# One byte copied in place of a shift and a masked merge in the narrowing of 64-bit weights, with a new order of all operations

## The chip, the cores and the metric

One core of a Trainium2 chip runs the whole program in one launch. The metric is the device time of an execution in microseconds, and less is better. The kernel is written for the engines directly: TensorE (PE) multiplies, VectorE (DVE), ScalarE (ACT) and GpSimd (POOL) do the elementwise work, and SyncE (SP) issues the DMAs.

## The reference, cut to what matters

Three layers run one after the other on 2 x 768 tokens:

```
attn:  q, k, v (2, 8, 768, 64): a window of +-15 keys, and 24 key sums (max over 32 keys) and value
       sums (mean) as extra columns; softmax; times v
moe:   x @ w_gate (4 experts, best 2 kept); q, k, v = x @ wq, wk, wv; causal softmax attention for
       every expert; times wo; the two kept experts are added with their softmaxed gates
moe2:  xk, xr = mixes of x and the previous token; k = max(xk @ w_k, 0); v = k*k @ w_v
       r = sigmoid(xr @ w_r); out = r * v
```

The three weights of the last layer, `w_k` (512 x 1024), `w_v` (1024 x 512) and `w_r` (512 x 512), reach the kernel as 64-bit floats, two 32-bit words each. The other inputs are 32-bit floats.

## The kernel before

The program builds a list of 2056 operations, each with the engines that could do it (its "ways"), and then issues them in an order written out by hand in `ORDER`. An entry is 4 times the number of the operation plus the number of the way: 770 is operation 192 in its third way, which is POOL. Each engine runs its own operations in that order and waits only where an operation needs another engine's result. `HOMES` gives the buffer slot of each tile. So `ORDER` sets which engine does what, and who queues behind whom; the costs written beside the operations were used to make it and are not read at run time.

The work has three stages. First the windowed attention (`stage1_*`, lines 570 to 700), tile by tile of 128 tokens. For a tile, PE makes the scores (line 583, or lines 588 and 589 for the first three tiles), DVE adds the mask and takes the maximum (line 606), ACT takes the exponentials (line 609), DVE sums and inverts (lines 612 and 614), any of three engines normalizes (lines 620 and 625), PE transposes (line 637), DVE and ACT copy the result out of PSUM (lines 368 and 369), and PE multiplies by the values (line 679). The value sums are copied into the value tiles (lines 534, 535 and 537) before that last product. Then the projections (lines 754 and 772) and the experts' attention (lines 854, 952, 994), interleaved with the rest of the first stage. Last the third layer: `w_r` (line 1146), `w_k` (line 1197) and `w_v` (line 1284), the last two as products of halves that save one multiplication in eight.

Every product of the second and third stage is made of three matmuls of rounded parts: a value x is split into a rounded high part and the low rest, by `halves` (a rounding copy, then a subtraction). PE is used in four shapes: whole (the projections and the last stage), by rows (lines 637 and 854), by halves (lines 679 and 952) and by quarters (lines 500, 583, 588, 589). A wait of PE at a step of the start is met by the operations of that step: the first projection, operation 256 (line 772), needs the high and low part of tile 0 (operations 124 and 125) and of its weight (29 and 30); operations 257 and 258 need 31 to 34. Operation 194, the value product of tile 2, needs the copies 192 and 193 of the value sums.

`raw64` (line 1014) makes 32-bit floats out of 64-bit ones. There are 20 pieces of 128 x 512 weights, four of `w_r`, eight of `w_k` and eight of `w_v`. For each piece it loads pairs of words, takes the magnitude of the high word, scaled (ACT, line 1035), bounds it (DVE or POOL, lines 1037 and 1038), shifts the low word right by 29 so that its last three bits are left (DVE, line 1041), merges the sign of the high word in (DVE, line 1043), and shifts the magnitude left by 3 and merges the two (DVE, line 1045). The split into parts follows.

Of the kernel before, what the change touches and what calls it, by code (L numbers as in the profile page):

```python
# [45 lines left out]
SIGN = -0x80000000  # L46
# [9 lines left out]
    12, 0, 4, 16, 36, 44, 24, 32, 56, 52, 64, 20, 60, 236, 72, 40, 92, 48, 244, 201, 68, 28, 188, 280, 100, 792,  # L56
    240, 650, 284, 272, 1238, 296, 108, 276, 206, 380, 304, 256, 300, 248, 288, 96, 308, 264, 1242, 292, 104, 646,
    210, 252, 260, 328, 268, 512, 440, 80, 408, 444, 400, 432, 404, 312, 464, 316, 412, 392, 332, 324, 424, 436,
    416, 76, 652, 384, 396, 548, 564, 428, 320, 572, 112, 336, 516, 388, 340, 532, 524, 420, 472, 88, 704, 790, 556,
    552, 468, 448, 540, 528, 452, 84, 344, 696, 348, 568, 456, 476, 576, 148, 352, 712, 356, 544, 680, 460, 560,  # L60
    360, 796, 216, 368, 480, 373, 365, 664, 520, 960, 484, 604, 536, 600, 622, 688, 489, 168, 1244, 580, 584, 848,
    590, 592, 613, 492, 976, 672, 656, 618, 1288, 609, 824, 1264, 748, 220, 117, 744, 132, 140, 496, 624, 121, 228,
    125, 1272, 136, 500, 773, 232, 129, 757, 1024, 770, 629, 760, 1028, 753, 764, 1032, 840, 144, 808, 1268, 856,
    776, 844, 632, 154, 812, 816, 676, 1036, 157, 780, 1048, 860, 1052, 162, 784, 820, 1056, 1060, 1296, 828, 164,
    1280, 1072, 668, 1068, 832, 1076, 708, 1304, 964, 1080, 716, 1164, 174, 1040, 952, 684, 1256, 1084, 968, 800,
    660, 1188, 1092, 1276, 224, 180, 1192, 804, 177, 196, 852, 1212, 980, 184, 192, 836, 1140, 212, 1088, 700, 1248,
    1144, 932, 864, 1044, 1252, 868, 1148, 877, 880, 692, 1152, 1260, 740, 872, 720, 724, 1064, 1168, 1300, 1157,
    1284, 1216, 728, 956, 3596, 1308, 1332, 1292, 1336, 596, 1160, 1506, 1357, 1172, 1312, 1316, 1220, 736, 1341,
    972, 732, 1326, 984, 1176, 1349, 504, 1196, 1362, 1353, 1180, 1224, 1344, 1501, 1525, 1320, 1200, 1229, 884,
    1520, 888, 1184, 1204, 892, 946, 1232, 1364, 904, 1208, 901, 948, 908, 897, 1852, 1369, 913, 1476, 1096, 1376,  # L70
    918, 1856, 1480, 1380, 1832, 1860, 1485, 938, 1489, 1528, 1497, 1864, 1372, 940, 1492, 1964, 1836, 1868, 1812,
    1572, 1840, 3600, 920, 1540, 992, 1968, 1844, 1816, 3605, 1556, 1824, 1548, 1508, 1820, 924, 1564, 1972, 1588,
    1828, 1580, 1384, 1552, 1532, 928, 1512, 1544, 2004, 1388, 1516, 1568, 988, 1584, 3608, 1576, 1104, 2192, 1000,
    1420, 1592, 1444, 2196, 3612, 1848, 2168, 1536, 1412, 3628, 1404, 1392, 1428, 2216, 2008, 1468, 1448, 2172,
    1560, 1436, 636, 1100, 1408, 2012, 2176, 640, 1109, 1432, 1396, 2180, 1472, 1872, 1596, 1400, 3616, 1612, 1924,
    2016, 1928, 1117, 1904, 1900, 1941, 3622, 1424, 2185, 996, 1416, 1004, 1917, 8, 1112, 1908, 3692, 1600, 1120,
    1936, 2188, 2200, 1912, 1328, 1009, 1440, 3640, 2204, 508, 1124, 3644, 2220, 2208, 1452, 1604, 2224, 1021, 1932,
    1876, 1944, 1128, 1456, 1976, 2212, 1984, 1017, 1608, 3632, 1672, 1988, 1013, 2020, 1992, 1787, 1464, 2760,
    1996, 1724, 1700, 1692, 1980, 1647, 1132, 1921, 1764, 2000, 1137, 1760, 1732, 1460, 1684, 2228, 1696, 1708,
    1791, 2024, 2768, 1769, 2240, 1776, 1880, 1756, 1712, 2764, 2244, 3624, 1780, 2248, 2028, 2776, 2233, 2252,  # L80
    1716, 1736, 1676, 1886, 2236, 1651, 2772, 1620, 2056, 2257, 1624, 1773, 2052, 3636, 1616, 1680, 2380, 3704,
    1629, 3648, 1640, 2068, 1948, 2033, 1633, 2400, 3654, 2432, 2072, 2065, 1636, 2416, 1688, 2038, 2384, 1728,
    1888, 3656, 1704, 1652, 1893, 1720, 2424, 2408, 2388, 1740, 2392, 1792, 1896, 1744, 1668, 2440, 1656, 1752,
    1952, 2060, 2260, 2444, 2080, 1808, 2076, 1796, 1660, 1748, 2780, 1664, 2396, 1800, 2464, 2092, 2512, 2096,
    1958, 1804, 2788, 2084, 2088, 2404, 3660, 2784, 2792, 3696, 4444, 2540, 2472, 2800, 2468, 2428, 4540, 2820,
    2524, 3701, 2548, 2481, 2796, 2477, 2100, 2484, 2812, 2556, 2488, 2572, 2564, 2436, 2828, 2576, 2516, 2816,
    2492, 3708, 2532, 2116, 2412, 2804, 3712, 2832, 2420, 2808, 2824, 1960, 2040, 2264, 2836, 2268, 2048, 2840,
    2560, 3718, 2272, 2536, 2844, 2312, 2448, 2497, 2044, 3720, 2276, 2848, 2852, 2316, 2452, 2104, 2320, 2500,
    2856, 2288, 2292, 2281, 2324, 2544, 2296, 2552, 2329, 2916, 2284, 2568, 3672, 2912, 2892, 2460, 2888, 2933,
    3028, 2929, 2904, 2332, 2921, 2520, 2925, 2456, 2968, 2908, 2964, 3032, 2896, 2900, 2300, 2981, 3036, 4448,  # L90
# [1397 lines left out]
```

## Time and profile before

| | |
|---|---|
| time, median of 3 runs | 333.66 us (333.64 to 333.79) |
| the profiled execution | 332.78 us, of which 331.0 us from its first to its last instruction |
| PE busy | 319.1 us, 96% |
| DVE busy | 311.3 us, 94% |
| ACT busy | 266.8 us, 81% |
| POOL busy | 114.0 us, 34% |
| HBM | 30.16 MB read, 3.15 MB written |
| granted TensorE clock, 331.0 us | 1.000 |

The shares are averages over the stages. A busy PE may still have gaps between matmuls, since the ends of matmuls are modelled; whether it has any is seen from the time that a run of equal matmuls takes.

### The profile page before, as it was taken

The numbers are of one execution on the slowest core, as the hardware profiler recorded it, in microseconds if no ns is written. First come the engines' busy times: TensorE is split into PE (matmuls) and PEld (weight loads), VectorE is DVE, ScalarE is ACT, GpSimd is POOL, SyncE is SP. The second block draws the span as 40 slices with busy tenths as digits, with TensorE's granted clock in tenths as the row PEclk, the third lists the DMA queues.
The fourth block names the chain that finished last, engine by engine and source line by source line (L and its number), as shares of the span: only waits on it lengthen the run. The fifth ranks groups of instructions, "written<-read, shape, count | busy, mean of one in ns | idle before, by whom it ended". The sixth has DMA issues, their size and how long they took to land.

```text
span 331.0 us, 8978 instructions
## 1 busy us (share of the span) xinstructions
PE 319.1 (96%) x3296; PEld 286.8 (87%) x3296; DVE 311.3 (94%) x941; ACT 266.8 (81%) x777; POOL 114.0 (34%) x127
## 2 busy tenths in 40 slices
PE   3979999999999999999999999999999999999995
PEld 2869988888789879787776899999998899999995
DVE  3789999999999899989999999999999999999996
ACT  0989999999898779779887889889799988965360
POOL 0556872768303810432310001545036000360231
PEclk9999999999999999999999999999999999999999
DMA  7996985757242000111212001100050000021033
GB/s 247 400 395 204 305 301 189 270 152 248 92 137 64 4 0 10 59 63 65 87 43 63 3 4 61 63 0 3 0 183 10 0 0 2 18 79 52 0 113 128
DMA packets 19628, 34.08 MB, mean 103 GB/s; under 512 B 2080, under 2 KB 8480, under 8 KB 19584
## 3 DMA queue, kind: packets, MB, share of 16 engines
q1 hardware_dynamic: 19584, 33.51, 30.0%
q8 instruction: 26, 0.43, 0.5%
q14 instruction: 18, 0.15, 0.1%
HBM read 30.16 MB, written 3.15 MB: 101 GB/s over the span
## 4 chain that ended last, share of the span: by engine, by line
PE 94%; DVE 2%; DMA 2%; SPq 1%; issue 0%; ACT 0%; ACTq 0%
PE ps L1284 18%; PE ps L1197 18%; PE ps L754 11%; PE ps L1146 10%; PE ps L637 6%; PE ps L952 6%; PE ps L772 6%; PE ps L854 6%; PE ps L994 5%; PE ps L679 3%; PE ps L583 3%; DMA ks<-in_kS 2%; PE ps L588 1%; PE ps L500 1%; DVE w L606 1%; SPq L359 1%
## 5 line engine op out<-in xcount | busy, mean ns | idle before, releaser
L1284 PE MATMUL ps<-w,s 128*128 128x256 f32 x336 | 48.7, 281 | 0.0
L1284 PEld LDWEIGHTS ps<-w,s 128*128 128x128 f32 x336 | 43.9, 188 | 0.1
L1197 PE MATMUL ps<-b,w 128*128 128x384 f32 x216 | 40.3, 337 | 0.0
L1197 PEld LDWEIGHTS ps<-b,w 128*128 128x128 f32 x216 | 38.0, 188 | 0.1
L368 ACT ACTIVATE t<-ps 128x192 f32<-128x192 f32 (+1 forms) x108 | 30.9, 356 | 8.6 <-PE ps L637 4.2
L754 PE MATMUL ps<-b,w 128*128 128x384 f32 x192 | 36.6, 341 | 0.0
L1146 PE MATMUL ps<-w,b 128*128 128x512 f32 x144 | 35.8, 398 | 0.0
L754 PEld LDWEIGHTS ps<-b,w 128*128 128x128 f32 x192 | 33.2, 188 | 0.9 <-issue 0.4
L1146 PEld LDWEIGHTS ps<-w,b 128*128 128x128 f32 x144 | 26.5, 188 | 5.9 <-DVE gsum L820 0.2
L609 ACT ACTIVATE w<-w,nm 128x120 f32<-128x120 f32 x72 | 28.5, 407 | 0.9 <-DVE nm L606 0.7
L368 ACT ACTIVATE b<-ps 128x384 f32<-128x384 f32 (+4 forms) x50 | 23.8, 492 | 3.9 <-PE ps L994 1.6
L368 ACT ACTIVATE s<-u 128x512 fp32r<-128x512 f32 x24 | 14.8, 628 | 9.4 <-DVE u L1059 5.5
L1123 DVE SCALAR_TENSOR_TENSOR t<-b,mu,t 128x384 f32<-128x384 f32 x32 | 21.2, 681 | 0.8 <-ACT t L387 0.7
L854 PE MATMUL ps<-ks,b 64*128 64x384 f32 (+3 forms) x192 | 21.8, 342 | 0.0
L368 ACT ACTIVATE w<-ps 120x256 f32<-120x256 f32 (+2 forms) x49 | 19.7, 445 | 1.7 <-PE ps L1146 0.8
L952 PE MATMUL ps<-t,b 128*64 128x384 f32 (+2 forms) x144 | 20.7, 422 | 0.0
L376 DVE TENSOR_TENSOR b<-t,b 128x384 fp32r<-128x384 f32 x37 | 20.1, 567 | 0.5 <-ACT b L368 0.3
L772 PE MATMUL ps<-q,b 128*128 128x260 f32 x144 | 20.3, 290 | 0.2 <-DVE b L376 0.2
L772 PEld LDWEIGHTS ps<-q,b 128*128 128x128 f32 x144 | 18.2, 188 | 1.6 <-issue 0.5
L368 ACT ACTIVATE b<-t 128x384 fp32r<-128x384 f32 x38 | 19.0, 516 | 0.5 <-PE ps L1197 0.5
L994 PE MATMUL ps<-u,w 128*128 128x384 f32 x96 | 18.9, 338 | 0.0
L387 ACT ACTIVATE t<-b,omu 128x384 f32<-128x384 f32 x28 | 16.9, 613 | 2.2 <-PE ps L952 1.6
(202 smaller groups left out, 913.4 us busy)
## 6 DMA issues: line engine op xcount, KB each, us to landing
s<-in_wk SPq DMA_DIRECT2D x8, 512.0 KB, 4.0
s<-in_wv SPq DMA_DIRECT2D x8, 512.0 KB, 4.2
w<-in_vp SPq DMA_DIRECT2D x15, 256.0 KB, 6.5
w<-in_qT SPq DMA_DIRECT2D x12, 256.0 KB, 5.6
out_y<-t SPq DMA_DIRECT2D x24, 128.0 KB, 1.8
s<-in_wr SPq DMA_DIRECT2D x4, 512.0 KB, 5.7
s<-in_kS SPq DMA_DIRECT2D x6, 320.0 KB, 4.7
ks<-in_kS SPq DMA_DIRECT2D x4, 400.0 KB, 3.9
```

The costliest lines, as they stand in the source:

```text
L368: ways = [("act", act(n, sb), lambda: nc.scalar.activation(dst(), src(), AF.Copy)), ("dve", dve2(n) if sb else dve(n), lambda: nc.vector.t ...
L376: ways = [("dve", dve(n), lambda: nc.vector.tensor_tensor(dst(), a(), b().bitcast(F32), ALU.subtract), sb)]
L609: op("act", act(NK, True) + 186, lambda i=i, z=z, pr=pr, nm=nm: nc.scalar.activation(pr()[:, i], pr()[:, i], AF.Exp, bias=nm.t[:, i:i + 1] ...
L754: mm(p.t[:, :C], a[kc].t[:, cols], x.t[:, kc, :], start=(kc == 0 and i == 0), stop=(kc == KC - 1 and i == 2))
L772: mm(p.t[:, :260], x.t[:, kc, tok], a[kc].t, start=(kc == 0 and i == 0), stop=(kc == KC - 1 and i == 2))
L854: mm(ps[e2].t[:, :z - a], q1.t[r, x, tok], ks.t[r, y, a:z], start=n == 0, stop=n == 2)
L952: mm(acc.t[64 * e2:64 * e2 + 64, tq0 * P:(tq0 + cnt) * P], vv.t[:, kb, e * D:(e + 1) * D], th[e2].t[:, i0 * P:(i0 + cnt) * P], start=first ...
L994: mm(p.t[:, :C], a[ep].t[:, m * P:(m + 1) * P], x.t[:, ep, :], start=(ep == 0 and i == 0), stop=(ep == 1 and i == 2))
L1123: op("dve", dve(C) + 60, lambda: nc.vector.scalar_tensor_tensor(tmp(), cur(), mu.t[:, i:i + 1], tmp(), ALU.mult, ALU.add), r=rd, w=[(mb, m ...
L1146: mm(p.t, a.t[:, kc, tok], w[2](), start=(kc == 0 and i == 0), stop=(kc == KC - 1 and i == 2))
L1197: mm(p.t[:, :C], a[2]()[:, o:o + P], x.t[:, u, j], start=not (j or i), stop=j == 1 and i == 2)
L1284: mm(p.t[:, :256], x.t[:, u, j * P:(j + 1) * P], v[2]()[:, col:col + 256], start=not (j or i), stop=j == FC // 2 - 1 and i == 2)
```

## The change

Two edits, one in `raw64` and one in `ORDER` and `HOMES`.

In `raw64` a new operation copies the top byte of the low word over the lowest byte of the high word, after the magnitude has been taken from it. The three wanted bits then stand in the high word beside the sign, and one instruction with two steps (shift right by 5, and a mask for the sign and the last three bits) replaces the shift and the merge. So a piece still has five operations: magnitude, bound, byte copy, shift and mask, last merge. The byte copy may go to ACT, POOL or DVE.

```diff
-        def low():
-            return raw.t[:, :, 0]
-
...
-        op("act", act(512, True) + 60, lambda: nc.scalar.activation(ff(), high(), AF.Abs, scale=F64_SCALE),
+        op("act", 660, lambda: nc.scalar.activation(ff(), high(), AF.Abs, scale=F64_SCALE),
            r=[raw], w=[(fg, 0)])
...
-        op("dve", dve2(512), lambda: nc.vector.tensor_scalar(g(), low(), 29, None, ALU.logical_shift_right),
-           r=[raw], w=[(fg, 1)], lock=True)
-        op("dve", dve(512), lambda: nc.vector.scalar_tensor_tensor(
-            g(), raw.t[:, :, 1], SIGN, g(), ALU.bitwise_and, ALU.bitwise_or), r=[raw], w=[(fg, 1)], lock=True)
+        def half(i):
+            return raw.t.bitcast(mybir.dt.uint8)[:, :, i]
+
+        any_of("act", [("act", 680, lambda: nc.scalar.activation(half(4), half(3), AF.Copy)),
+                       ("pool", pool_ts(512), lambda: nc.gpsimd.tensor_copy(half(4), half(3))),
+                       ("dve", dve2(512), lambda: nc.vector.tensor_copy(half(4), half(3)), True)], w=[raw])
+        op("dve", dve2(512), lambda: nc.vector.tensor_scalar(g(), raw.t[:, :, 1], 5, SIGN + 7, ALU.arith_shift_right,
+                                                             ALU.bitwise_and), r=[raw], w=[(fg, 1)], lock=True)
```

`ORDER` and `HOMES` are new throughout. The list of operations is the same but for the two above. Of its 20 byte copies the new order gives 11 to ACT, 7 to POOL and 2 to DVE. 231 of the 2056 operations change their engine, in all directions, and the counts of operations go from 781 to 778 on DVE, 579 to 567 on ACT and 123 to 138 on POOL. PE has the same 458 operations; it changes between its four shapes 81 times instead of 87, and from operation 194 on (the same 26 operations of PE lie before it in both orders) 71 times instead of 78.

The start of the new order, up to operation 194 (entry 776), against the old (entry 776 too):

```diff
-    12, 0, 4, 16, 36, 44, 24, 32, 56, 52, 64, 20, 60, 236, 72, 40, 92, 48, 244, 201, 68, 28, 188, 280, 100, 792,
-    240, 650, 284, 272, 1238, 296, 108, 276, 206, 380, 304, 256, 300, 248, 288, 96, 308, 264, 1242, 292, 104, 646,
-    210, 252, 260, 328, 268, 512, 440, 80, 408, 444, 400, 432, 404, 312, 464, 316, 412, 392, 332, 324, 424, 436,
-    416, 76, 652, 384, 396, 548, 564, 428, 320, 572, 112, 336, 516, 388, 340, 532, 524, 420, 472, 88, 704, 790, 556,
-    552, 468, 448, 540, 528, 452, 84, 344, 696, 348, 568, 456, 476, 576, 148, 352, 712, 356, 544, 680, 460, 560,
-    360, 796, 216, 368, 480, 373, 365, 664, 520, 960, 484, 604, 536, 600, 622, 688, 489, 168, 1244, 580, 584, 848,
-    590, 592, 613, 492, 976, 672, 656, 618, 1288, 609, 824, 1264, 748, 220, 117, 744, 132, 140, 496, 624, 121, 228,
-    125, 1272, 136, 500, 773, 232, 129, 757, 1024, 770, 629, 760, 1028, 753, 764, 1032, 840, 144, 808, 1268, 856,
-    776, 844, 632, 154, 812, 816, 676, 1036, 157, 780, 1048, 860, 1052, 162, 784, 820, 1056, 1060, 1296, 828, 164,
...
+    12, 0, 16, 36, 44, 24, 32, 56, 52, 64, 20, 188, 236, 96, 40, 68, 48, 244, 205, 72, 28, 104, 209, 280, 60, 1238,
+    240, 284, 304, 650, 272, 92, 788, 202, 380, 276, 288, 248, 292, 256, 100, 264, 4, 260, 646, 296, 1242, 252, 108,
+    268, 308, 328, 512, 300, 432, 424, 436, 464, 408, 312, 400, 428, 316, 384, 412, 76, 652, 324, 440, 392, 444,
+    416, 556, 220, 388, 532, 794, 516, 420, 80, 472, 524, 320, 704, 396, 332, 548, 336, 564, 404, 112, 340, 572,
+    344, 520, 656, 448, 552, 452, 88, 348, 680, 352, 460, 540, 536, 664, 560, 712, 84, 356, 576, 468, 373, 456, 688,
+    528, 796, 148, 360, 368, 544, 672, 568, 365, 952, 476, 1244, 489, 486, 580, 960, 480, 584, 8, 696, 600, 840,
+    604, 590, 593, 168, 492, 1356, 216, 618, 1296, 613, 496, 622, 848, 609, 744, 808, 500, 748, 133, 196, 118, 624,
+    764, 137, 125, 224, 121, 773, 129, 1024, 142, 629, 757, 1028, 760, 753, 1032, 768, 660, 632, 144, 676, 776, 668,
...
```

In it the first slab copies on ACT are operations 51 and 52 instead of 50; the normalization 148 of tile 2 (entry 593) is on DVE instead of POOL, the copy 192 (entry 768) too; the roundings 33 and 35 of the first weights leave DVE for ACT and POOL, and the subtraction 34 comes to DVE from POOL.

## Rows read from the trace of the kernel before

**Rows 1.** The page, busy time of PE and DVE: us, share, instructions.
```profile
PE 319.1 (96%) x3296; PEld 286.8 (87%) x3296; DVE 311.3 (94%) x941; ACT 266.8 (81%) x777; POOL 114.0 (34%) x127
```
**Rows 2.** Windows: PE, PEld, DVE, ACT, POOL busy (instructions), clock, DMA share, GB/s.
```profile
30.00:45.00 15.00, 15.00 (x162) 14.15 (x160) 14.50 (x47) 14.19 (x61) 10.89 (x12) 1.00 0.85 286
...
210.00:225.00 15.00, 15.00 (x87) 15.00 (x86) 15.00 (x31) 12.35 (x28) 6.22 (x5) 1.00 0.00 1
```
**Rows 3.** The chain that ended last, from the first weights on: start us, us, what.
```profile
196.28 54.67 PE ps L1197 x312
...
266.91 2.85 PE ps L1284 x24
...
270.45 56.77 PE ps L1284 x480
327.25 0.43 DVE t L1170
327.70 0.43 DVE t L1059
```
**Rows 4.** Groups by shape: x count, busy us, mean ns, idle before.
```profile
L1043 DVE SCALAR_TENSOR_TENSOR s<-s,s 128x512 int32<-128x512 int32 x20 | 14.7, 736 | 0.0
L1035 ACT ACTIVATE s<-s 128x512 f32<-128x512 f32 x20 | 13.5, 684 | 1.3 <-POOL q L378 1.3
L1041 DVE TENSOR_SCALAR s<-s 128x512 int32<-128x512 int32 x20 | 8.5, 436 | 0.0
L371 POOL TENSOR_SCALAR w<-s 128x512 fp32r<-128x512 f32 x12 | 8.2, 685 | 4.2 <-DVE rse L885 2.3 <-DVE s L1045 1.7
L1038 POOL TENSOR_SCALAR s<-s 128x512 f32<-128x512 f32 x2 | 3.8, 1922 | 2.5 <-PE ps L637 1.4 <-ACT s L1035 1.1
L620 DVE TENSOR_TENSOR w<-w,rss 128x480 f32<-128x480 f32 x1 | 0.7, 657 | 0.0
```
**Rows 5.** Line 1045: ns least/median/most, first and last start in us.
```profile
L1045 DVE SCALAR_TENSOR_TENSOR s<-s x20: 675/688/1475, 54.6 to 260.5; 128x512 int32<-128x512 int32 x20
```
**Rows 6.** The chain, runs of equal matmuls with and without a change of shape.
```profile
37.83 0.61 PE ps L637 x16
...
44.22 0.47 PE ps L637 x16
...
100.24 2.10 PE ps L754 x12
...
106.88 2.30 PE ps L754 x12
```
**Rows 7.** Timeline of ACT, 9 to 11 us: start us, us, engine, line.
```profile
10.06 0.74 ACT L368 ACTIVATE s<-ks 128x640 f32<-128x640 f32 x1
```
**Rows 8.** The chain, 20 to 30 us.
```profile
20.50 0.72 DVE w L534
...
24.33 0.42 DVE q L369 x2
24.74 0.91 DVE q L376
...
25.86 0.61 DVE b L376
26.51 1.53 PE ps L772 x9
28.05 1.08 PE ps L679 x32
```
**Rows 9.** Timeline of DVE, 23 to 28 us, with the idle time before an instruction.
```profile
23.63 0.28 DVE L606 CUSTOM_DVE_ANT_0 w<-ps,msk 128x120 f32<-128x120 f32 x1 [0.74 <-PE ps L583]
...
24.66 1.00 DVE L376 TENSOR_TENSOR q<-b,q 128x260 fp32r<-128x260 f32 x1
...
26.39 0.73 DVE L376 TENSOR_TENSOR q<-b,q 128x260 fp32r<-128x260 f32 x1
```
**Rows 10.** Timeline of POOL, 24 to 27 us.
```profile
24.62 0.75 POOL L378 TENSOR_TENSOR q<-b,q 128x260 fp32r<-128x260 f32 x1 [1.16 <-DVE q L369]
```

260 rows, old and new, of tables (HOMES, ORDER) are left out of this document.

## Prediction

> **What bounds the kernel now.** Three views, in this order. The page's busy shares give PE 96% and DVE 94% [rows 1], which leaves open which of the two sets the end. The windows narrow it: between 30 and 45 us, and again between 210 and 225 us, PE is busy for all of 15.00 us, and DVE for 14.50 and 15.00 us [rows 2]. A busy PE can still hide gaps, so the third view decides, the chain that ended last. In it 312 matmuls of 384 columns take 54.67 us, 0.175 us each, and 480 of 256 columns take 56.77 us, 0.118 us each [rows 3]. The same 0.175 us holds far ahead of that stage: 12 matmuls of line 754 take 2.10 us at 100.24 us [rows 6], when DVE's queue holds quite other work. A rate that is the same in stages with different company is PE's own rate, not a wait on DVE. So from about 29 us to 327.25 us PE runs back to back, and what is left outside are the start (PE reaches its first projection at 26.51 us and waits between its runs before that) [rows 8] and the end: two DVE instructions of 0.43 us [rows 3] and the last DMA, up to 331.0 us.
>
> From this follows the rule for all that comes: an edit is worth what it changes in the length of PE's own queue, in the start, or in the end. A saving on DVE is worth nothing unless PE waited for it.
>
> **The change in raw64.** It takes away 20 merges of line 1043, 0.736 us each, 14.7 us of DVE [rows 4]. The shift of line 1041 (0.436 us) becomes a shift with a mask on the same tile; I leave its price at 0.436 us, since the words read and written are as many. It adds 20 byte copies of 128 x 512. None is in the trace, so bounds: the nearest row for ACT is line 1035, which reads the same pairs of words (0.684 us); for POOL line 371 with 0.685 us below and line 1038 with 1.922 us above; for DVE 0.436 us of line 1041 below and 0.736 us of line 1043 above [rows 4]. I take 0.68 us on ACT, 0.69 on POOL (a copy is nearer to line 371 than to the bounding of line 1038) and 0.44 on DVE. That gives 11 x 0.68 = 7.5 us more on ACT, 7 x 0.69 = 4.8 us on POOL, 2 x 0.44 = 0.9 us on DVE. The new order then moves other work: 781 operations of DVE become only 778, so most of the 14.7 us is filled again.
>
> On the path to the end this is worth 0. What hides it is PE itself, saturated. The new copy also lengthens the chain of one piece, since it must wait for the magnitude, and the shift for the copy: at most 0.68 + 0.44 = 1.1 us [rows 4], less what the bound beside them takes. The cover: the last piece's line 1045 starts at 260.5 us [rows 5], and its stage begins on PE at 266.91 us [rows 3], which leaves 6.4 us for the merge and the splits behind it. If that cover were gone, it would cost 1.1 us once.
>
> **PE's queue in the new order.** PE has the same 458 operations, so only the changes of shape differ. Their price: 16 transposes of line 637 take 0.61 us with a whole-array run behind them and 0.47 us with a run by rows behind them, and 12 matmuls of line 754 take 2.30 us after transposes and 2.10 us among their like [rows 6]. So a change costs between 0.14 and 0.20 us. From operation 194 on the new order has 71 changes where the old has 78. 7 x 0.14 = 0.98 us less; with 0.20 it would be 1.4 us, and nothing if the new places make PE wait. I take 0.98 us, the nearer price for a change by itself, because only about half of the changes enter a whole-array run.
>
> **The start.** In both orders the same 26 PE operations come before operation 194 (line 679, at 28.05 us now), so it is a fair mark. DVE sets it. Up to the subtraction 125 (25.86 us now) both queues hold, from the first reduction of line 612 on, 25 maxima, 3 reductions with their reciprocals, 4 copies of value sums, 2 copies of transposes and one copy of line 534. The old one holds besides two weight roundings (0.42 us) and a subtraction (0.91 us) [rows 8]; the new one a normalization (0.66 us) [rows 4]. That is 0.42 + 0.91 - 0.66 = 0.67 us earlier. Against it, ACT makes two slab copies ahead of the exponentials of tile 0 and not one; a copy holds ACT for 0.64 us (10.06 to 10.70; the row's 0.74 us overlaps the next) [rows 7], so the first reduction starts 0.64 us later. The two cancel. The idle 0.74 us of DVE at 23.63 us [rows 9] may go or stay, since the scores that ended it stand earlier in PE's queue now.
>
> Behind 125 the new DVE queue is longer: 125 itself, the subtractions 34, 30 and 32, the rounding 157, and the copy 192, for which PE's operation 194 waits. With 0.61 us for a large one [rows 8], 0.65 us for a subtraction of weights undisturbed (0.73 us in the row, less the overlap) [rows 9] and 0.72 us for line 534 [rows 8]: 0.61 + 3 x 0.65 + 0.61 + 0.72 = 3.89 us. From 25.86 us this ends at 29.75 us, 1.70 us after the 28.05 us at which PE starts operation 194 now; without DVE's idle time (0.74 us, and 0.28 us spread ahead of it) it would end at 28.73 us, 0.68 us later. I take 0.6 us as the loss, near that lower end, because the wait at 23.63 us came from scores that PE now has done by then. Both ends stay: a gain of some 0.4 us, if DVE is as early and the three subtractions interleave better, to a loss of 1.7 us. What is late next is DVE's operation 158, for operation 262 of PE; the 1.08 us of operation 194 [rows 8] hide its 0.61 us.
>
> **The end.** The new order also closes with a sum and a product on DVE after the last PE operation. The last but one operation of PE leaves DVE the same two, 2 x 0.43 us [rows 3], which fit into the last one's 12 x 0.118 = 1.4 us. So 0 us, and no more than 0.9 us late if DVE came with two instructions of arrears.
>
> **Sum.** Against the profiled execution's 332.78 us (331.0 us of span and 1.8 us around it): 0 - 0.98 + 0.6 + 0 = -0.4 us, 332.4 us. The median of the runs shown is 333.66 us, 0.9 us above that execution, so the forecast for it is 333.3 us. That is 0.1% faster, and what a measurement of this kernel can tell from no change is about 0.2%, 0.67 us: forecast no change.
>
> **Rivals.**
> The start costs nothing: the copy 192 comes in time and only the changes of shape count, 333.66 - 0.98 - 0.3 = 332.4 us. For it: DVE loses its 0.74 us wait. Against: 3.89 us of DVE's work stand between the start of 125 and operation 194, where now operation 194 starts 2.2 us behind it (25.86 to 28.05 us) [rows 8].
>
> DVE was the bound after all: then part of 14.7 us comes back. In the rows DVE is idle for nothing at 210 to 225 us [rows 2], so it can't be excluded by its own share; the equal 0.175 us speaks against it. With one in seven of the 14.7 us on the path, 333.3 - 2.1 = 331.2 us; I give it less than a tenth.
>
> Slower, by POOL's byte copy: if it is like line 1038, 1.92 us, a copy is 1.23 us above my price. Five of the seven stand early, beside PE's runs between about 45 and 105 us, when POOL also makes the normalizations that PE waits for soonest. Between 30 and 45 us POOL is idle for 4.1 us [rows 2], so one or two are absorbed; where two stand directly ahead of a normalization PE waits 2 x 1.23 = 2.5 us: 333.3 + 2.5 = 335.8 us. It decides once such a copy is longer than about 1.4 us, twice line 371. Against it: a copy has no arithmetic, and the two calls of line 1038 in the old order did no harm.
>
> Slower, by DVE and POOL at once: of two equal subtractions of line 376 one took 1.00 us [rows 9] while POOL's line 378 ran beside it [rows 10], the other 0.73 us [rows 9], and line 1045 has a median of 688 ns and a most of 1475 ns [rows 5]. With 0.27 us more for each of the three subtractions of the start and 0.27 us for the copy 192, the loss there is 0.6 + 1.08 = 1.7 us: 333.66 - 0.98 + 1.7 = 334.4 us. POOL has 15 operations more. The Trainium skill has a rule for it (GPSIMD Engine Reference, "8. Key points"): GpSimd shares its SBUF interfaces with VectorE, and they contend when VectorE reads two inputs from SBUF or runs in a mode with both ports. By that rule, the change removes 20 two-input instructions and adds 7 GpSimd ones; the rows agree that such a slowdown exists.
>
> That the bits are not as meant (the mask cut to the sign alone) would change the result's last bits and no time.
>
> **How the numbers follow.** Forecast case, 333.3 us, its own range 332.6 to 334.0 us: 0.50, of which 0.10 faster, 0.38 the same, 0.02 slower. Start free: 0.20, 0.19 of it faster and 0.01 the same. DVE bound: 0.08, faster. POOL copy: 0.10, slower. DVE beside POOL: 0.12, of which 0.09 slower and 0.03 the same. So faster 0.37, same 0.42, slower 0.21. The range leaves out DVE as the bound (0.08) and the POOL copy's upper part (0.10): 332.0 to 334.9 us.
>
> **What would show it.** PE again at 0.175 and 0.118 us a matmul in the long runs, and no line 1043 of a merge: DVE busy down by only a few us, ACT's about the same. The run of line 679 before the long projections at 28.7 us, held by DVE's line 534. POOL's byte copies at 0.7 us, ACT's at 0.68 us. From there on less than 1 us gained to the last matmul, which then ends near 326.9 us, and 3.8 us from it to the end. The prediction is wrong if PE's idle time appears between 30 and 185 us, if the byte copies on POOL pass 1.4 us, or if the long runs of PE themselves get shorter per matmul.

## The result, and the profile after

The new kernel takes 335.48 us (median of 6 runs, 335.16 to 336.59) where the kernel before takes 333.65 us beside it (332.56 to 334.64). The ratio is 1.0064, 95% interval 1.0039 to 1.0089: it is 0.6% slower. The forecast was 333.3 us and no change, with a range that ended at 334.9 us.

The profiled execution has a span of 333.6 us, 2.6 us more than before. First the busy times of its page, in the form of [rows 1]:

```profile
PE 318.0 (95%) x3296; PEld 287.4 (86%) x3296; DVE 310.1 (93%) x938; ACT 274.7 (82%) x763; POOL 119.7 (36%) x142
```

DVE was relieved of 14.7 us of merges and yet has only 1.2 us less to do. The windows, with the columns of [rows 2], show two of its stretches again and two later ones:

```profile
30.00:45.00 15.00, 15.00 (x168) 14.31 (x164) 14.41 (x53) 14.46 (x64) 8.58 (x10) 1.00 0.71 229
210.00:225.00 15.00, 15.00 (x87) 15.00 (x86) 15.00 (x32) 12.85 (x28) 5.55 (x4) 1.00 0.00 0
220.00:240.00 20.00, 20.00 (x116) 20.00 (x115) 20.00 (x42) 19.14 (x40) 6.54 (x6) 1.00 0.08 27
240.00:260.00 20.00, 19.24 (x98) 17.14 (x97) 19.93 (x39) 18.03 (x35) 3.78 (x4) 1.00 0.16 54
```

The last stretch in the kernel before:

```profile
240.00:260.00 20.00, 20.00 (x103) 18.30 (x102) 20.00 (x43) 19.33 (x42) 8.23 (x4) 1.00 0.25 80
```

Where nothing waits, PE keeps its pace (87 matmuls in 15 us, as in [rows 2]). Between 240 and 260 us it is idle for 0.76 us, where it was never idle before, while DVE is busy for 19.93 of the 20. So DVE and PE are both full there, and a late DVE shows. The groups by shape, as in [rows 4]:

```profile
L1040 ACT ACTIVATE s<-s 128x512 uint8<-128x512 uint8 x11 | 15.2, 1379 | 0.2
L1045 DVE SCALAR_TENSOR_TENSOR s<-s 128x512 int32<-128x512 int32 x20 | 14.1, 708 | 0.1
L1031 ACT ACTIVATE s<-s 128x512 f32<-128x512 f32 x20 | 13.6, 684 | 0.7 <-DVE s L1043 0.7
L1041 POOL COPY s<-s 128x512 uint8<-128x512 uint8 x7 | 9.8, 1393 | 5.4 <-ACT s L1031 2.7 <-issue 2.5
L1043 DVE TENSOR_SCALAR s<-s 128x512 int32<-128x512 int32 x20 | 9.4, 469 | 1.5 <-ACT s L1040 0.7 <-POOL b L987 0.4 <-POOL s L1041 0.3
...
L1042 DVE COPY s<-s 128x512 uint8<-128x512 uint8 x2 | 1.5, 748 | 0.0
```

A byte copy costs 1.38 us on ACT, 1.39 on POOL and 0.75 on DVE, about twice what I had put in on each engine. On DVE it costs what the removed merge cost (0.736 us). The chain that ended last, in the form of [rows 3], is no longer PE's at the end but DVE's, back to where the view could follow it:

```profile
322.14 1.43 DVE t L1059
323.57 0.60 DVE s L375
...
329.52 0.42 DVE t L1059
329.94 0.34 DVE t L1170
330.29 0.02 issue
330.31 0.42 DVE t L1059
```

The timeline of PE in three places (start, length, and in brackets the idle time before it with what ended it):

```profile
27.81 1.45 PE L771 MATMUL ps<-q,b 128*128 128x260 f32 x9
29.50 1.15 PE L678 MATMUL ps<-w,u 120*64 120x64 f32 x32 [0.24 <-DVE u L533]
...
95.57 0.80 PE L753 MATMUL ps<-b,w 128*128 128x384 f32 x3 [0.47 <-DVE nm L860]
...
325.71 2.99 PE L1284 MATMUL ps<-w,s 128*128 128x256 f32 x24
```

With these rows the 2.6 us of this pair of executions split into three. Operation 194 starts at 29.50 us where it was 28.05 us [rows 8]: +1.45. From there to PE's end (327.22 us before, 328.70 us after) it takes 299.20 us (328.70 less 29.50) where it took 299.17 (270.45 + 56.77 less 28.05) [rows 3, 8]: +0.03. From PE's end to the end of DVE's last instruction it takes 2.03 us (330.73 less 328.70) where it took 0.91 [rows 3]: +1.12.

The +0.03 in the middle is no sign that nothing happened there. The windows from operation 194 to PE's end, first before, then after:

```profile
28.05:327.22 299.17, 299.16 (x2831) 270.25 (x2831) 291.40 (x840) 249.15 (x709) 101.59 (x103) 1.00 0.25 80
29.50:328.70 299.20, 297.98 (x2831) 270.50 (x2831) 289.00 (x837) 256.51 (x694) 107.88 (x117) 1.00 0.24 78
```

PE's busy time became 1.18 us shorter (299.16 to 297.98 us), and PE now stands idle for 1.22 us, where it stood idle for 0.01 us. The 1.22 us are three waits: 0.47 us at 95.57 us, 0.52 us at 243.02 us (ended by ACT, whose copy before had itself waited 0.31 us for DVE's line 1045) and 0.24 us at 252.61 us. The timelines of POOL and DVE in the new kernel say what happens to DVE:

```profile
92.56 1.37 POOL L1041 COPY s<-s 128x512 uint8<-128x512 uint8 x1
93.74 1.02 POOL L377 TENSOR_TENSOR u<-t,u 128x384 fp32r<-128x384 f32 x1
...
239.14 1.64 POOL L377 TENSOR_TENSOR w<-s,w 128x512 fp32r<-128x512 f32 x1 [1.75 <-ACT w L367]
...
321.99 1.29 POOL L377 TENSOR_TENSOR s<-b,s 128x512 fp32r<-128x512 f32 x1 [4.93 <-ACT s L367]
```

```profile
93.96 1.07 DVE L1043 TENSOR_SCALAR s<-s 128x512 int32<-128x512 int32 x1 [0.27 <-POOL s L1041]
...
239.08 0.54 DVE L375 TENSOR_TENSOR b<-t,b 128x384 fp32r<-128x384 f32 x1
239.55 1.65 DVE L1123 SCALAR_TENSOR_TENSOR t<-b,mu,t 128x384 f32<-128x384 f32 x1
...
322.06 1.51 DVE L1059 TENSOR_TENSOR t<-t,w 128x256 f32<-128x256 f32 x1
```

Lay the two side by side. At 322.06 us a DVE product that takes 0.42 us elsewhere starts 0.07 us behind a POOL subtraction and takes 1.51 us: it ends 0.29 us after POOL does. At 239.55 us another ends 0.42 us after POOL's. Such an instruction makes little headway until POOL is done. In the whole trace of the new kernel 44 DVE instructions with two SBUF inputs start with more than 0.2 us of a POOL instruction still to run, and 19 of them are more than 0.15 us longer than the median of their shape; of the 75 that read PSUM and start so, none is. The Trainium skill states this as an exclusive lock (SBUF — State Buffer, "Who interferes with whom"): of the pair of ports that VectorE and GpSimd share, the engine that issues first keeps it for its whole instruction and the other is blocked when VectorE runs in a mode with both ports, and VectorE with two SBUF inputs contends with a GpSimd instruction that reads SBUF. The trace agrees, at 1.51 us against 0.42; the subtraction there is the only POOL instruction between 318 and 327 us. Where POOL's instruction comes second, it is POOL that waits: its product at 264.66 us takes 5.21 us, where one of the same shape at 249.27 us takes 0.73 us, and DVE's subtractions beside it keep their 0.68 us. Most of the 25 that were not held stand beside such a waiting POOL instruction.

```profile
264.66 5.21 POOL L1060 TENSOR_TENSOR s<-s,s 128x256 f32<-128x256 f32 x1 [14.66 <-DVE s L1059]
```

By 95.57 us it has reached PE: the shift with mask waits for POOL's byte copy (0.27 us), is held by POOL's next subtraction (1.07 us for 0.42), the maximum of line 860 behind it is late, and PE waits 0.47 us.

### The profile page after: what moved, and what is told of

It reads as the page before. It is cut to its first block, busy times and chain, and to the rows that moved or that the text cites. A ratio compares the mean times of both kernels' runs of the same rounds, so it can differ in the third digit from the quotient of the medians.

```text
span 333.6 us, 8972 instructions
## 1 busy us (share of the span) xinstructions
PE 318.0 (95%) x3296; PEld 287.4 (86%) x3296; DVE 310.1 (93%) x938; ACT 274.7 (82%) x763; POOL 119.7 (36%) x142
## 5 line engine op out<-in xcount | busy, mean ns | idle before, releaser
L1197 PE MATMUL ps<-b,w 128*128 128x384 f32 x216 | 41.0, 338 | 0.5 <-ACT b L367 0.5
L753 PE MATMUL ps<-b,w 128*128 128x384 f32 x192 | 37.1, 341 | 0.5 <-DVE nm L860 0.5
L367 ACT ACTIVATE t<-ps 128x192 f32<-128x192 f32 (+1 forms) x94 | 27.3, 343 | 4.7 <-PE ps L636 3.5
L608 ACT ACTIVATE w<-w,nm 128x120 f32<-128x120 f32 x72 | 27.7, 394 | 0.0
L377 POOL TENSOR_TENSOR b<-t,b 128x384 fp32r<-128x384 f32 x7 | 8.4, 1201 | 38.3 <-ACT b L367 38.3
L1060 POOL TENSOR_TENSOR t<-t,w 128x256 f32<-128x256 f32 x7 | 9.8, 1398 | 31.2 <-DVE t L1059 11.1
L375 DVE TENSOR_TENSOR b<-t,b 128x384 fp32r<-128x384 f32 x37 | 20.9, 574 | 0.0
L367 ACT ACTIVATE w<-ps 120x256 f32<-120x256 f32 (+2 forms) x47 | 18.6, 438 | 1.9 <-PE ps L1146 0.9
L377 POOL TENSOR_TENSOR w<-s,w 128x512 fp32r<-128x512 f32 x12 | 16.4, 1364 | 10.2 <-ACT w L367 7.3
L993 PE MATMUL ps<-u,w 128*128 128x384 f32 x96 | 19.7, 341 | 0.0
L853 PE MATMUL ps<-ks,b 64*128 64x384 f32 (+3 forms) x192 | 19.5, 335 | 0.0
```

The lines of the kernel that those rows point to most:

```text
L367: ways = [("act", act(n, sb), lambda: nc.scalar.activation(dst(), src(), AF.Copy)), ("dve", dve2(n) if sb else dve(n), lambda: nc.vector.t ...
L375: ways = [("dve", dve(n), lambda: nc.vector.tensor_tensor(dst(), a(), b().bitcast(F32), ALU.subtract), sb)]
L377: ways.append(("pool", pool_tt(n), lambda: nc.gpsimd.tensor_tensor(dst(), a(), b().bitcast(F32), ALU.subtract)))
L608: op("act", act(NK, True) + 186, lambda i=i, z=z, pr=pr, nm=nm: nc.scalar.activation(pr()[:, i], pr()[:, i], AF.Exp, bias=nm.t[:, i:i + 1] ...
L753: mm(p.t[:, :C], a[kc].t[:, cols], x.t[:, kc, :], start=(kc == 0 and i == 0), stop=(kc == KC - 1 and i == 2))
L993: mm(p.t[:, :C], a[ep].t[:, m * P:(m + 1) * P], x.t[:, ep, :], start=(ep == 0 and i == 0), stop=(ep == 1 and i == 2))
```

## The experiments

Theories. A: the byte copy's double price. B: the new order's start. C: DVE is a bound beside PE, so what is added to it shows. D: C, and POOL takes from DVE beside it as much as it takes off it. E: the new order's count of DVE work alone. Every ratio is to the kernel before, timed on the same chip. The kernel before had medians of 333.65 to 334.05 us beside these runs, so two kernels that were not timed side by side are better compared by their ratios than by their medians; where the two differ, both are given. The new kernel has 1.0064 (1.0039 to 1.0089).

**The copy at the price assumed (e1_word_copy).**

```diff
-            return raw.t.bitcast(mybir.dt.uint8)[:, :, i]
+            return raw.t[:, :, 1].bitcast(F32)
```

> The new kernel with its order, but each of the 20 copies takes the high word onto itself (4 bytes an element, 128x512) and not one byte; left out: the three last bits of the low word, so the last bits of the weights are not the reference's. The instruction count, the engines and the waits stay. Theory A (the byte copy's price: 1.38 us on ACT, 1.39 on POOL, 0.75 on DVE in the new kernel, twice what I had put in): the word copy takes 0.7 us on ACT and POOL and 0.4 on DVE, the waits of PE at 94, 242 and 252 us and the late DVE at the end go, and the time falls by 1.0 to 2.6 us from the new kernel's 335.5 us, to 332.9 to 334.5 us. Theory B (the order itself: its start, 1.5 us later at operation 194, and DVE's arrears at the end): the copies get cheaper but the time stays within 0.5 us of 335.5 us.

Measured: 335.10 us, 1.0027 (1.0003 to 1.0052). The groups and PE at 95 us:

```profile
L1042 ACT ACTIVATE s<-s 128x512 f32<-128x512 f32 x11 | 7.5, 686 | 0.2
L1043 POOL COPY s<-s 128x512 f32<-128x512 f32 x7 | 4.9, 704 | 5.2 <-ACT s L1033 2.7 <-issue 2.5
```

```profile
95.13 0.80 PE L755 MATMUL ps<-b,w 128*128 128x384 f32 x3
```

The wait at 95 us is gone, those at 242 and 252 us and the late end stay. The intervals of the two ratios overlap, so the 0.4% between them is a likely part of the loss and not proved by this run.

**The edit alone (e2_old_order_new_edit).** Old `ORDER` and `HOMES`, the copy issued right behind its magnitude:

```diff
-    ... 900 (magnitude) ... 902 (shift) ... 903 (merge) ...
+    ... 900 (magnitude), 902 (byte copy) ... 903 (shift with mask) ...
```

> The old order and homes with the new raw64: the byte copies stand right behind their magnitude, on the same engines as in the new order (11 ACT, 7 POOL, 2 DVE), and the shift with mask stands where the merge stood. DVE loses 20 x 0.736 us of merges and gains 2 x 0.75 us. Theory A (byte copy's price): ACT gains 15 us and POOL 10 us in an order that has no room made for them, and the time rises to 334.5 to 337 us. Theory B (the order): the edit by itself costs and brings nothing, 333.2 to 334.0 us, as the kernel before (333.65 us). Theory C (DVE is a bound after all): its 13 us less show as a gain, below 333.0 us.

Measured: 347.72 us, 1.0416 (1.0381 to 1.0450). All three theories missed the size. By its page DVE is busy for 303.2 of 345.2 us, idle for 42.0, where it was idle for 19.7 before [rows 1]. The place that shows how, POOL, DVE and PE at 61 to 65 us:

```profile
61.32 1.31 POOL L1043 COPY s<-s 128x512 uint8<-128x512 uint8 x1 [1.63 <-issue]
```

```profile
62.66 1.06 DVE L1045 TENSOR_SCALAR s<-s 128x512 int32<-128x512 int32 x1 [2.55 <-DMA w<-in_qT]
```

```profile
64.12 0.96 PE L855 MATMUL ps<-ks,b 64*128 64x512 f32 x5 [2.14 <-DVE nm L862]
```

The bracket names a DMA, but the instruction starts as POOL's copy ends (62.63 us): that copy it waited for. Before, shift and merge needed only the load and ran whenever DVE's queue came to them; now DVE stands still in its queue until another engine has copied, and PE behind it. The edit is not free by itself: in the old order, with the copy put right behind its magnitude, it costs 14 us.

**The order alone (e3_new_order_old_edit).** Shift and merge of the old `raw64` in the new order.

```diff
-        any_of("act", [... half(4), half(3) ...], w=[raw])
-        op("dve", ... 5, SIGN + 7, ALU.arith_shift_right, ALU.bitwise_and) ...
+        op("dve", ... raw.t[:, :, 0], 29, None, ALU.logical_shift_right) ...
+        op("dve", ... g(), raw.t[:, :, 1], SIGN, g(), ALU.bitwise_and, ALU.bitwise_or) ...
```

> The new order and homes with the old raw64: shift and merge on DVE, no byte copies. Against the new kernel ACT loses 15 us and POOL 10 us of copies and DVE gains 20 x 0.736 - 2 x 0.75 = 13.2 us. Theory A (byte copy's price on ACT and POOL): the waits for ACT at 242 and 252 us go, 333.0 to 334.5 us, as DVE's share of 93% leaves room. Theory B (the order's start): no change from the new kernel, 335.2 to 335.8 us. Theory C (in the new order DVE has no room, as its 2.2 us behind the last matmul say): PE waits for DVE in the stretch of the weights and the time rises by 3 to 13 us, to 338.5 to 348 us.

Measured: 345.03 us, 1.0331 (1.0299 to 1.0363), theory C's range. From 200 to 250 us its windows give

```profile
200.00:250.00 50.00, 46.98 (x266) 46.02 (x264) 49.72 (x93) 40.74 (x86) 16.14 (x12) 1.00 0.07 22
```

3 us of PE idle beside a full DVE. Of 13.2 us more on DVE, 9.6 us came out as time by the medians (345.03 less 335.48), 8.9 us by the ratios. In this kernel DVE has little room left.

**Bounds left out (e5_no_bound_new, e6_no_bound_old).** The other direction: DVE's load made less.

```diff
-        any_of("dve", [("dve", dve2(512), lambda: nc.vector.tensor_scalar(ff(), ff(), F64_TOP, None, ALU.min), True),
+        any_of("dve", [("dve", dve2(512), lambda: None, True),
```

> The new kernel without the 18 bounds of the magnitude that its DVE makes (line 1033, 0.488 us each, 8.8 us; 5 of them, 2.1 us, behind 199 us, where DVE is never idle). Left out: the bound, which only acts on weights out of range. Theory C (DVE paces the last third of the new kernel: it ends 2.2 us behind the last matmul, and PE waits for it at 242 and 252 us): the time falls by 1.0 to 2.5 us, to 333.0 to 334.5 us. Theory B (only the start, then PE's own queue): 335.1 to 335.6 us.

> The kernel before without the 18 bounds on DVE (line 1037, 0.42 us each, 7.5 us; 5 of them, 2.0 us, behind 199 us). My first step, that PE's queue is the bound there and a saving on DVE is worth nothing: 333.3 to 334.0 us, as the kernel before. Theory C, carried to the kernel before (DVE busy for 20.00 of 20.00 us there too, and so a bound as much as PE): 331.5 to 332.8 us.

Measured: 334.77 us, 1.0019 (1.0000 to 1.0037), and 333.58 us, 0.9978 (0.9960 to 0.9997). The new kernel, with 8.8 us less on DVE, gains 0.7 us by the medians, between the two forecasts, and 0.45% or 1.5 us by the ratios, theory C's range; the two intervals do not overlap. The kernel before, with 7.5 us less on DVE, gains 0.2%: my first step nearly held there. Saving on DVE brings a sixth of it or less, adding to it costs two thirds or more.

**The start (e4_old_start, e8_old_start_mended).**

```diff
-    12, 0, 16, 36, 44, 24, 32, 56, 52, 64, 20, 188, ...   (new, up to entry 776)
+    12, 0, 4, 16, 36, 44, 24, 32, 56, 52, 64, 20, 60, ... (old, up to entry 776)
```

> The new kernel, but with the old order, engines and load order for the operations in front of operation 194 (the same operations stand there but for nine, which follow at their new places), everything behind it as in the new kernel. Theory B (the start costs 1.5 us): operation 194 starts near 28.0 us and not 29.5, and the time falls by 1.0 to 1.5 us, to 334.0 to 334.5 us. Theory A (the copies' price decides; the later waits for ACT and DVE take back what the start gains): 335.0 to 335.6 us, with the waits at 94, 242 and 252 us longer.

Measured: 341.57 us, 1.0224 (1.0192 to 1.0257). The trial broke what it tested: operation 339 came early, its load late.

```profile
33.46 1.94 PE L773 MATMUL ps<-q,b 128*128 128x260 f32 x7 [5.01 <-DVE b L377]
```

It shows one thing all the same. While PE waits, the granted clock falls to half, 1.2 GHz (0.50 from 30.5 to 37 us); operation 194 starts at 35.76 us, 6.3 us later than in the new kernel, and the time is longer by 6.1 us by the medians (341.57 less 335.48), 5.3 us by the ratios. Little of such a loss is taken back later.

> The new kernel behind the old start again (order, engines and loads of the operations in front of operation 194), this time with the load and the value-sum copy of operation 339 (lines 474 and 535) put where DVE does not wait for them, which held DVE and PE for 5 us in the first trial. Theory B (the start costs the new kernel 1.5 us): operation 194 starts near 28.0 us, and the time is 333.9 to 334.6 us. Theory C (DVE paces the last third, and a start that gives PE 1.5 us gives DVE the same): the same 333.9 to 334.6 us, but with DVE again 2 us behind PE at the end. If neither holds: 335.2 us and more.

Measured: 334.62 us, 1.0001 (0.9977 to 1.0025); operation 194 at 28.87 us. That is below the new kernel, by 0.9 us by the medians and 2.1 us by the ratios, and the two intervals do not overlap: the old start is the faster one. DVE ends 2.0 us behind PE, as theory C has it; e9 finds another cause for that. How much the start costs is less clear, since it varies between executions: in all profiles but e4's operation 194 starts at 28.7 to 30.3 us with the new start (eight, mean 29.4) and 27.2 to 30.1 us with the old (ten, mean 28.8), a difference of 0.6 us. But these means mix two clocks. In two of the eight and in six of the ten the granted TensorE clock falls to half, 1.2 GHz, for a part of 22 to 29 us. It did not in the first pair. The windows of the kernel before and of e6, which has the same start:

```profile
22.00:26.00 4.00, 3.47 (x104) 3.18 (x106) 3.26 (x17) 3.14 (x9) 2.85 (x4) 1.00 1.00 352
22.00:26.00 4.00, 3.39 (x62) 3.08 (x62) 2.20 (x14) 1.72 (x6) 1.79 (x3) 0.57 0.86 297
```

Without the fall the means are 29.1 us (new start, six) and 27.8 us (old, four), with it 30.3 us (two) and 29.5 us (six). At like clock the new start is thus later by 1.3 or 0.8 us, more than the predicted 0.6 us, and the 1.45 us of the first pair is near the first of these. The groups are small, and the starts in them differ by up to 1.3 us.

**POOL's late work on DVE (e7_late_pool_on_dve).**

```diff
-    1481, 1746, 1751, 1773, 1770, 1831, 1822, 1864, 1921, 1970 on POOL
+    1481, 1746, 1751, 1773, 1770, 1831, 1822, 1864, 1921, 1970 on DVE, at the same places
```

> The new kernel, but ten two-input operations of its last third go from POOL to DVE, at their places in the order: the ones beside which the trace shows a DVE instruction 0.43 to 0.97 us longer than its like (5.9 us in all). On DVE they take 8 x 0.42, 0.55 and 0.69 us, 4.6 us. Theory D (DVE is the bound of the last third, and POOL beside it takes from DVE more than it takes off it): the time falls by 0.3 to 1.3 us, to 334.2 to 335.2 us, although DVE has ten instructions more. Theory C without D (DVE is the bound, POOL's help is free): it rises by 3 to 4.6 us, to 338.5 to 340 us. Theory B (PE's queue alone): 335.2 to 335.8 us.

Measured: 335.35 us, 1.0024 (1.0007 to 1.0042). Ten instructions, 4.6 us, were added to a DVE that is full, and the time did not rise (0.1 us less by the medians; 1.3 us less by the ratios, which is theory D's range, but the intervals just meet), where e3's 13.2 us had raised it by 9 us or more. That excludes theory C without D. The median is in theory B's range as well, but e3 has shown that DVE's load counts. POOL's help on these ten was worth no time that shows.

**The end (e9_end_order).**

```diff
-    1990, 2051, ..., 1996, 2027, 2031, 2038, 2032, ...   (operations of DVE, in order)
+    1996, 2027, 2038, 2031, 1990, 2051, 2032, ...
```

> The new kernel with one move in DVE's queue near the end: at 322 us it makes four sums that read PSUM (operations 1996, 2027, 2038, 2031) ahead of the product 1990 and the subtraction 2051, so that none of DVE's operations with two SBUF inputs stands beside POOL's subtraction 2044 (321.99 to 323.28 us), beside which 1990 took 1.51 us and not 0.42. Nothing is added or removed. Theory D (POOL holds such a DVE instruction until it is done, and that is the 1.1 us by which the new order ends later behind its last matmul): the last DVE instruction ends 1.1 to 1.3 us behind the last matmul and not 2.2, and the time falls by 0.8 to 1.2 us, to 334.3 to 334.8 us where the new kernel has 335.5 us. Theory E (DVE is late there by its count of instructions, whatever stands beside it): still 2.2 us, 335.2 to 335.8 us.

Measured: 334.52 us, 1.0014 (0.9988 to 1.0039). POOL, DVE and PE at the end:

```profile
321.50 1.30 POOL L379 TENSOR_TENSOR s<-b,s 128x512 fp32r<-128x512 f32 x1 [4.93 <-ACT s L369]
```

```profile
321.56 0.75 DVE L1300 TENSOR_TENSOR t<-ps,t 128x256 f32<-128x256 f32 x2
...
323.19 0.41 DVE L1061 TENSOR_TENSOR t<-t,w 128x256 f32<-128x256 f32 x1
...
328.84 0.43 DVE L1061 TENSOR_TENSOR t<-t,w 128x256 f32<-128x256 f32 x1
```

```profile
325.21 2.99 PE L1286 MATMUL ps<-w,s 128*128 128x256 f32 x24
```

The sums that read PSUM are not held beside the same POOL subtraction, the product behind it takes 0.41 us again, and DVE ends 1.07 us after PE (329.27 less 328.20), not 2.03. In all six kernels with the new end and POOL's work untouched it is 2.0 to 2.1 us, in all with the old or the mended end 0.9 to 1.1. The end's 1.1 us is POOL's one subtraction, beside a two-input instruction. The order of four instructions mends all but 0.15 us of it.

**The waits at 242, 252 and 94 us (e10_end_and_two, e11_and_old_start, e13_end_and_94, e14_all_waits).** On top of e9:

```diff
-    1481, 1751 on POOL                    (e10; e11 adds the old start)
+    1481, 1751 on DVE
-    918 on POOL                           (e13, from e9; e14, from e11)
+    918 on DVE
-    1551, 1678 on DVE                     (e14)
+    1551, 1678 on ACT
```

> As the last, and two subtractions (1481 at 203 us, 1751 at 239 us) go from POOL to DVE, where they take 0.55 and 0.69 us; beside them on POOL a DVE instruction took 0.83 and 0.97 us more than its like. Theory D: PE's wait at 242 us (0.86 us) goes, and the time falls by 0.3 to 0.9 us from the kernel with the end alone. Theory E: DVE has 1.2 us more to do where it is never idle, and the time rises by 0.5 to 1.2 us from it.

Measured: 334.72 us, 1.0017 (0.9995 to 1.0039). The product of line 1125 at 239.99 us takes 0.61 us again and the wait at 242 us is gone; PE's next wait grew:

```profile
253.15 1.19 PE L1148 MATMUL ps<-w,b 128*128 128x512 f32 x4 [0.60 <-DVE b L1172]
```

It was 0.24 us in the new kernel, and a wait of 0.51 us at 47.5 us is new. In all, PE is idle for 1.7 us between operation 194 and its end, where it is idle for 1.2 us in the new kernel and in e9. The wait that was mended came back elsewhere; that this is because DVE has as much to do in all is my reading, and no run separates it from the spread between executions.

> As the last, with the old start in front (the mended one: operation 194 at 28.9 us there, 28.0 to 29.1 us with the old start in four profiles, 28.7 to 30.2 us with the new one in five). If start and end add up: 0.7 us less than the last kernel, 333.0 to 333.8 us, no slower than the kernel before. If what the start gains is lost again on the way: the same as the last kernel within 0.3 us.

Measured: 334.26 us, 1.0019 (0.9998 to 1.0040): beside e10 the old start shows nothing that the interval can tell, unlike e8 beside the new kernel. Operation 194 starts at 28.56 us, where it was 28.85 us in e10.

> The new kernel with the end mended (as in e9_end_order) and one byte copy, operation 918 at 92.6 us, moved from POOL to DVE. In the new kernel the shift with mask behind it waits 0.27 us for POOL and then takes 1.07 us beside POOL's next subtraction, and PE waits 0.47 us for the maximum behind it (line 860). Theory D (the new edge from POOL to DVE, and POOL beside DVE): DVE gives 0.74 us and gets back 0.27 + 0.65 us, PE's gap of 0.69 us at 94 us goes, and the time is 0.3 to 0.7 us below e9_end_order's 334.5 us. Theory E (DVE's count of work sets it): 0.5 to 0.8 us above.

Measured: 335.19 us, 1.0037 (1.0016 to 1.0059). Not below e9. PE's wait at that place, idle time as in the brackets, fell from 0.47 us to 0.16 us (at 96.36 us), without a gain in time that shows. Theory E's rise fits the ratios better, but the intervals of e9 and e13 overlap. That place stays open beyond what e1 showed of it.

> Old start, mended end, the subtractions 1481 and 1751 and the byte copy 918 on DVE, and two copies that DVE makes at 243.7 and 251.3 us (operations 1551 and 1678, 0.47 and 0.27 us) on ACT instead. If the new order's saving of 0.98 us on changes of shape is real and only DVE's waits hid it: PE's gaps at 94, 242 and 252 us are gone or under 0.4 us, and the time is 332.6 to 333.6 us, 0.1 to 0.4% below the kernel before. If the waits only move on: 334.0 to 334.6 us as with the old start and mended end alone.

Measured: 334.04 us, 1.0002 (0.9982 to 1.0023), no faster than before: the second forecast, that the waits move on. PE is still idle for 1.1 us behind operation 194.

**The copy's price again, and what sets it (e12_and_two_bytes, e15_all_waits_word_copy, e16_byte_to_word, e17_word_to_byte).** In e12 the copy is one 16-bit element (from e11); the others are e14 with

```diff
-        nc.scalar.activation(half(4), half(3), AF.Copy)
+        nc.scalar.activation(word, word, AF.Copy)       (e15)
+        nc.scalar.activation(word, half(3), AF.Copy)    (e16)
+        nc.scalar.activation(half(4), word, AF.Copy)    (e17; word = raw.t[:, :, 1] as 32-bit float)
```

> As the last, and the copy takes the upper two bytes of the low word over the lower two of the high word, as one 16-bit element (the shift is then by 13); the weights come out as in the reference. If an element's price is the same for 16 bits as for 32 (0.69 us on ACT, 0.70 on POOL in the trial with whole words): 0.7 us a copy, PE's wait at 94 us goes, 0.2 to 0.5 us less than the last kernel. If every element below 32 bits costs double: 1.4 us a copy and no change.

> As e14_all_waits with each copy taking the high word onto itself (32 bits an element); left out: the three last bits of the low word. Theory A (the byte copies' double price costs PE time also where the waits are mended): 0.3 us or more below e14_all_waits. Theory D (their price is hidden beside PE once no DVE instruction waits for one on POOL): the same within 0.3 us.

> e14_all_waits with each copy reading the byte and writing it as a 32-bit number over the high word; left out: signs and last bits of the weights. Same count of elements and the same stride. If the price comes from writing below 32 bits: 0.69 us on ACT and 0.70 on POOL, 0.42 on DVE. If from reading: 1.38, 1.39 and 0.74 us.

> e14_all_waits with each copy reading the high word as a 32-bit number and writing one byte; left out: the last bits of the weights. If the price comes from writing below 32 bits: 1.38 us on ACT, 1.39 on POOL, 0.74 on DVE. If from reading: 0.69, 0.70 and 0.42 us.

Measured: e12 335.45 us, 1.0038 (1.0017 to 1.0060); e15 333.09 us, 0.9985 (0.9964 to 1.0006); e16 and e17 one execution each, for the price. The groups of e12, of e16 and of e17:

```profile
L1042 ACT ACTIVATE s<-s 128x512 uint16<-128x512 uint16 x11 | 15.1, 1374 | 0.2
```

```profile
L1042 ACT ACTIVATE s<-s 128x512 f32<-128x512 uint8 x11 | 7.5, 686 | 0.2
L1043 POOL CAST s<-s 128x512 f32<-128x512 uint8 x6 | 4.2, 704 | 5.7 <-ACT s L1033 3.2 <-issue 2.5
L1044 DVE CAST s<-s 128x512 f32<-128x512 uint8 x3 | 1.3, 422 | 0.0
```

```profile
L1042 ACT ACTIVATE s<-s 128x512 uint8<-128x512 f32 x11 | 15.1, 1375 | 0.2
L1043 POOL CAST s<-s 128x512 uint8<-128x512 f32 x6 | 8.4, 1394 | 5.8 <-ACT s L1033 3.2 <-issue 2.5
L1044 DVE CAST s<-s 128x512 uint8<-128x512 f32 x3 | 2.2, 748 | 0.0
```

The write doubles the price, on all three engines, and 16 bits are as dear as 8; e12's interval overlaps e11's, so no change is shown there. Reading a byte costs what reading a word does. e15 is 0.17% below e14 by the ratios (0.6 us), 0.95 us by the medians of the same chip, theory A's forecast; with e1 against the new kernel (0.37%) that is two trials in one direction, and neither interval stands clear alone. My estimate for what the copies' double price costs in time, from these two, is between 0.5 and 1.2 us. No kernel that does the whole computation beats the kernel before.

## Why the prediction was wrong, step by step

The step that failed is the one that put DVE's delays at nothing: "On the path to the end this is worth 0. What hides it is PE itself, saturated." Against the forecast's four terms the first pair of profiles has, in us:

| term | forecast | measured |
|---|---|---|
| PE's waits for DVE in the middle | 0 | +1.22 |
| PE's own queue behind operation 194, as busy time | -0.98 | -1.18 |
| the start | +0.6 | +1.45 |
| the end | 0 | +1.12 |
| sum | -0.4 | +2.6 |

The medians differ by 1.83 us and the ratio stands for 2.1 us; the pair is a little wider than both.

- **PE bounds, a saving on DVE is worth nothing.** Nearly right for savings in the kernel before (e6: 0.2%). What I drew from it was wrong: PE hides little that DVE does late. [rows 2] had DVE at 15.00 of 15.00 us; I wrote "so it can't be excluded by its own share", where it means that a delay of DVE has no slack there (e3: 9 of 13.2 us came out as time). The new order made such delays: a wait for POOL's copy at 94 us, and DVE instructions held beside POOL at 94, 239 and 322 us. My estimate from the traces, each such instruction less the median of its shape: POOL holds DVE for 10.6 us in the kernel before and for 14.0 us in the new one.
- **The copies' prices.** 0.68, 0.69 and 0.44 us were put in; 1.38, 1.39 and 0.75 came. ACT had no upper bound in my text, DVE's came just above my upper bound, POOL's inside the two: I went by the words read, and the write decides (e16, e17). By e1 and e15 it cost 0.5 to 1.2 us, of which the wait at 95 us is a part.
- **The longer chain of a piece, at most 1.1 us, covered by 6.4.** The cover was counted to the stage that uses the weights. The wait came instead in DVE's queue, for what stands behind the shift: at 94 us in the new kernel, and at 62.66 us in e2.
- **PE's changes of shape, -0.98 us.** The size came out near: PE's busy time behind operation 194 is 1.18 us less. In the kernel before and in e6, with the old order, it is 299.2 us; in fifteen profiles with the new one it is 297.9 to 299.3 us (median 298.4), and in e3, full of waits, 302.1 us, so some waiting may be counted as busy too. No run separates the changes of shape from the rest of the order. PE's waits took the gain back; the step had said "nothing if the new places make PE wait", and that bound was the case.
- **The start, +0.6 us.** What was late is what I named: operation 194 waits for line 533 of DVE. The size was short: 0.8 or 1.3 us at like clock, 1.45 us in the first pair. That the mean over all eighteen profiles comes to 0.6 us is luck, since more of the old start's profiles had the fall of the clock.
- **The end, 0, at most 0.9 us.** 1.12 us. I had the right two instructions and the arrears as the bound, and not what makes arrears: one POOL subtraction 6 us ahead (e9).
- **The rivals.** POOL's byte copy was to decide above 1.4 us; it came to 1.39 and held PE by 0.5 us, not 2.5. Its 335.8 us is near the measured time by luck. DVE beside POOL, put at the start with 1.1 us, was the mechanism elsewhere: at 94, 242 and 322 us (e10 and e9 mend the last two); at 252 us it is not shown.
- **The signs.** Of the three that I named one came: PE's idle time between 30 and 185 us, 0.47 us at 95.57 us. The long runs kept their pace, and POOL's copies stayed a hair under 1.4 us.

What is open: how the middle's 1.22 us divide between the copies' price and POOL beside DVE, since a wait taken away at one place came back at another (e10, e14), and the size of the start (e8 against e11).

## What to carry to other kernels

Where two engines are both busy for all of a stretch, a saving on one brings little (here a sixth of it or less) and a delay of either shows (here two thirds of it or more), so price what an edit delays before what it removes. Count POOL's instructions beside full DVE stretches at their price for DVE: a DVE instruction with two SBUF inputs that starts behind POOL's was held here until POOL was done (1.51 us for 0.42), and sums that read PSUM are what to put there. Compare two starts only at the same granted clock. A write of elements below 32 bits, eight bytes apart, cost about twice a 32-bit one on ACT, POOL and DVE; read the narrow element, and write a whole word if the algorithm allows it.

## What was not expected of the hardware

Writing 128 x 512 bytes, or 16-bit elements, eight bytes apart takes 1.37 to 1.40 us on ACT and POOL and 0.75 on DVE, where 32-bit elements at the same places take 0.69, 0.70 and 0.42 us; the width that is read makes no difference. And a DVE instruction with one input can be held too: the shift with mask at 93.96 us took 1.07 us beside POOL where most of its like take 0.42 (407, 418 and 1075 ns least, median and most).
